# One layer's weight conversions name an activation table set, the order's model opens with no set loaded, and the plan's constants change with it

## The chip, the cores and the metric

The kernel runs on one core of a Trainium2 chip. The time is the device time of one execution in microseconds, the median of several runs. The core has five engines that run side by side, each taking its own instructions in order: PE (TensorE, matrix products), DVE (VectorE), ACT (ScalarE), POOL (GpSimd) and SP (SyncE, which here only issues DMAs). They wait for each other by semaphores. Data lie in SBUF (128 partitions), products in eight PSUM banks.

## The reference

Three steps follow each other; `B, H, S, D = 4, 8, 768, 48`, so there are 3072 tokens of 384 features.

```python
for t in range(S):                                   # attention with a decaying state
    state = alpha[:, :, t, :, None] * state + k_t v_t^T
    y[:, :, t] = q_t . state
h = x @ w_in                                         # layer one, 384 -> 2048 -> 384
P = a[0] + a[1] * h + a[2] * h2 + a[3] * h3          # h2 = h * h, h3 = h2 * h
Q = 1.0 + np.abs(b[0]) * np.abs(h) + np.abs(b[1]) * h2
x = (P / (Q + 1e-06)) @ w_out
h = x @ w_in2                                        # layer two, same sizes
out = (h * np.tanh(softplus(h))) @ w_out2
```

The weights arrive as 64-bit floats, so each is read as pairs of 32-bit words and made into two 32-bit parts, a high one in PE's reduced format and a low rest. Activations are split alike, and each product is the sum of three matmuls (high by high, high by low, low by high).

## The kernel before

**Tiling.** Tokens go in six chunks of 512 (128 positions of each of four batches). Attention works a chunk as two units (`attn_unit`): a tree of decay products, six levels of small score matmuls (L462) with a masked copy behind each (L497, or L486 and L492 on ACT) and a scaling of queries and keys (L477), then transposes (L526), outer products (L541), a state update (L550 on POOL, L555 on DVE) and the outputs (L576, L612). A layer works a chunk as 16 steps, one for each 128 of the 2048 hidden features. A step has nine hidden matmuls of 128x512 (L653) into one of three banks, the nonlinear function (`hidden`), a split of its result into high part `gh` and low part `gl` (`split_g`) and nine output matmuls (L702) that add into three banks over the 16 steps.

**Phases.** A pair (layer, chunk) is a phase. `PHASES` gives their order: (0, 0), (0, 1), (1, 0), (0, 2), (1, 1) and so on, layer two following layer one by a chunk. The attention of chunk c + 1 is worked beside the phases before layer one needs it; that of chunk 0 stands ahead of everything. Layer one's function takes ACT's logarithm and exponential, layer two's its Mish; these belong to two table sets, and ACT loads one at each change of layer (L690, L800; 1283 ns each). The first load, L731, stands in `start`.

**The order.** No order is written out by hand. Each operation is entered in a `Plan` with its engine, a length, a due time, the keys it reads and writes, and the code that emits it. `Plan.order` simulates the engines: when one is free, it takes the operation with the earliest due time of those that are ready. The sequence that results is what is emitted, for each engine in that order. So due times only rank what is ready, but one length that changes can change who is ready first, and with that the rest of the sequence. ACT operations may name a table set; where it isn't the one that the simulation holds loaded, their length is taken 1.4 us longer (line 157). Matmuls with constants (`warm`, L746) that feed nothing are put in where PE is idle until a set point; a trace shows 120 of them.

**Weight conversions.** `load_w` brings a pair of weight blocks in (L327 on SP) and converts it: ACT scales the high words (L328); then in form `A` of `E_CV` ACT makes two more pieces (L341, L342) and DVE joins them (L344), in form `D` DVE does three operations (L330, L332, L334). `E_HC` says whether ACT (L221) or DVE (L223) casts the high part, `E_LW` who makes the low part. Conversions 0 to 15 are layer one's, 16 to 31 layer two's. For later chunks the results are kept in DRAM and streamed back (`stream`, eight buffers each).

**Who does what.** Strings with a letter for each chunk give engines: `E_M` the multiplication in layer one's function (`V`: L671 on DVE, `P`: L675 on POOL), `E_GL0` and `E_GL1` the subtraction for `gl` in layer one and two (L214 on DVE, L216 on POOL). `T_PH` spaces the due times of a phase's steps, `AT_P` places the attention units, `D_SPL` and `LAG` place the split and the output matmuls behind a step, `W_LEAD` and `X_LEAD` the loads of streamed weights and of layer two's input, `D_W2` layer two's conversions, `D_X` the split of the inputs, `D_EV` the copies out of the output banks.

Of the kernel before, what the change touches and what calls it, by code (L numbers as in the profile page):

```python
# [14 lines left out]
AF = mybir.ActivationFunctionType  # L15
# [21 lines left out]
NLVM = 5  # L37
T0 = 24.974
PHASES = ((0, 0), (0, 1), (1, 0), (0, 2), (1, 1), (0, 3), (1, 2), (0, 4), (1, 3), (0, 5), (1, 4), (1, 5))
T_PH = (8.402, 4.683, 4.572, 7.535, 7.065, 5.706, 9.463, 9.341, 5.182, 6.904, 4.724, 3.344)  # L40
AT_P0 = (0.318, -13.418, 0.649)
AT_P1 = (0.292, 1.189, 0.288)
AT_P = (0.573, 0.916, 0.31)
D_MID = 10.219
LAG = (32.081, 10.172)
D_SPL = (-7.368, 6.936)
W_LEAD = 4.738
X_LEAD = 96.57
D_W1 = (0.495, 18.655)
D_W2 = (17.835, 18.763)  # L50
E_LO = 'VV'
E_TREE, E_QK = ('PPPVPV', 'VVVVVP')
E_M = 'PPPPPV'
E_GL0 = 'PVVPVV'
E_GL1 = 'VVVVPV'
R_PSUM = 'R.....'
NWL, NWO = 8, 8
N16 = 20
C_PED = 2
N_PRE = 8  # L60
E_LW = 'PVPPPVVVVVVVVVVVVVVVVVVVVVVVVVVV'
E_HC = 'AAVVVVVVAAVAAAAVVVAVAVAAVVVAVAAA'
E_X0 = 'V'
E_CV = 'ADAAAAAAAAAAADADDDDDADDDAAAAAAAA'
R0 = (39.706, 10.751)
NRAW, NF32 = 2, 2
D_X = 86.568
D_EV = -19.693
PAD_FROM = 290.0
PAD = 0.7  # L70
PAD_L = 0.5
F_OPEN = 3.25
F_END = 91.927
F_RATE = 1325.024
# [4 lines left out]
F64_SHIFT = 2.0 ** -112  # L79


class Plan:
# [32 lines left out]
    def order(self):  # L115
# [8 lines left out]
        ops = self.ops = list(ops)  # L124
        events = [(1.9, 1, n) for n in range(len(ops)) if not left[n]]
        heapq.heapify(events)
        out, busy, loaded = [], {}, "ln"
        fill, filler = self.fill, None
        while events:
            t = events[0][0]  # L130
            while events and events[0][0] <= t + 1e-9:
                _, kind, n = heapq.heappop(events)
# [13 lines left out]
            for eng, q in ready.items():  # L146
# [3 lines left out]
                while q:  # L150
                    due, n = heapq.heappop(q)
# [3 lines left out]
                    _, us, _, _, _, lock, after, table = ops[n]  # L155
                    if table and table != loaded:
                        us, loaded = us + 1.4, table
# [31 lines left out]
def attention_moe_kernel(ctx: ExitStack, tc: tile.TileContext,  # L189
                         qka, nat, consts, ab, w1i, w1o, w2i, w2o, out):  # L190
    nc = tc.nc
# [13 lines left out]
    def act(n, due, reads, writes, emit, src="p", ptr=0, table=None):  # L205
        plan.add("ACT", (0.075 if src == "p" else 0.115) + 0.000840 * n + 0.093 * ptr, due, reads, writes, emit, table=table)
# [101 lines left out]
    def load_w(src, l, key, j, due):  # L308

        n = nload[0]  # L310
        nload[0] += 1
        raw, st = raws[n % len(raws)], f32s[n % len(f32s)]
        kr, ks = f"raw{n % len(raws)}", f"f32{n % len(f32s)}"
# [11 lines left out]
        n = 2 * DM  # L325
        nth = nload[0] - 1
        dma(786, R0[nth] if nth < len(R0) else due - 6, [], [kr], lambda: nc.sync.dma_start(out=raw, in_=src[j]))  # L327
        act(n, due, [kr], [ks], lambda: nc.scalar.activation(st, mag, AF.Copy, scale=F64_SHIFT), src="s")  # L328
        if E_CV[nth] == "D":
            dve(n, due, [], [ks], lambda: nc.vector.tensor_scalar(  # L330
                out=si, in0=si, scalar1=3, scalar2=None, op0=ALU.logical_shift_left), fast=True)
# [556 lines left out]
```

## Time and profile before

| what | value |
|---|---|
| median of three runs | 1003.24 us (1002.68 to 1008.17) |
| the profiled execution | 1004.26 us, span 1001.6 us |
| PE busy | 969.1 us, 97% of the span |
| DVE, ACT, POOL busy | 668.6, 622.4, 263.6 us |
| DMA, mean over the span | 200 GB/s |
| mean granted TensorE clock | 0.989 |

The span is the time from the first instruction's start to the last one's end on the core; the execution's own time is 2.7 us longer. A row of busy time by stretch gives the stretch in us from the span's start, its length, the busy time of PE, PEld (weight loads of PE), DVE, ACT and POOL, each with its count of instructions, then the mean granted clock as a share of full speed, the DMA engines' busy share and GB/s. A row of the timeline gives the start, the duration, the engine, the line, the operation with what it writes and reads, and in brackets the idle time of the engine before it and who ended it ("issue": nothing that the profile shows). A row of waits gives who waited for whom, the total in us, how often, and the longest. A row of a group gives its busy time, the mean ns of one, and the idle time before it. The first hidden matmul of the phases, in order, starts at 85.48, 174.50, 257.10, 342.13, 409.41, 492.09, 560.89, 646.52, 719.17, 798.09, 859.06 and 928.42 us, and the stretches are cut there.

### The profile page before, as it was taken

Reading aid. Unit: us, or ns where it says so; the run is one execution under the profiler, and the core shown is the slowest. Engines: PE = TensorE matmul, PEld = TensorE weight load, DVE = VectorE, ACT = ScalarE, POOL = GpSimd, SP = SyncE. Lnnn points to the kernel's source line nnn. Section 1 sums busy time; section 2 is a strip of 40 time slices with the busy share of each in tenths; the row PEclk is TensorE's granted clock in tenths of the full one; section 3 lists DMA queues with packets and bytes.
Section 4 is the critical chain, followed back from the end, with each engine's and each line's share of the span. In section 5 each row is a group of like instructions: output and inputs, shape, how many; then the busy total and the mean of one; then the engine's idle time right before and its main releaser. Section 6 shows DMA issues by size and latency. Waiting matters only on the chain.

```text
span 1001.6 us, 24480 instructions
## 1 busy us (share of the span) xinstructions
PE 969.1 (97%) x10376; PEld 784.4 (78%) x10376; DVE 668.6 (67%) x867; ACT 622.4 (62%) x1051; POOL 263.6 (26%) x202
## 2 busy tenths in 40 slices
PE   7998999899999999999999999999999999999998
PEld 5776877678788878788878888878788878888886
DVE  5668799999997789954589634699952389400211
ACT  2587999699969698622399723396621299633332
POOL 3023675454100044200277700153300000133000
PEclk9799999999999999999999999999999999999999
DMA  7266549756588868557736764848456454565530
GB/s 293 98 222 270 199 151 326 252 164 206 203 292 311 309 230 277 173 191 225 255 97 222 228 210 135 293 153 263 117 167 190 143 156 143 142 214 150 172 111 31
DMA packets 75756, 199.98 MB, mean 200 GB/s; under 512 B 8192, under 2 KB 34944, under 8 KB 74112
## 3 DMA queue, kind: packets, MB, share of 16 engines
q1 hardware_dynamic: 75648, 198.43, 60.3%
q8 instruction: 81, 1.33, 0.5%
q14 instruction: 27, 0.22, 0.1%
HBM read 166.94 MB, written 31.46 MB: 198 GB/s over the span
## 4 chain that ended last, share of the span: by engine, by line
PE 68%; DVE 11%; ACT 9%; issue 3%; DMA 3%; POOL 1%; DVEq 0%; ACTq 0%; POOLq 0%
PE bank L702 31%; PE bank L653 30%; PE pair L462 4%; DVE zp L686 2%; DVE zp L677 1%; DVE zp L679 1%; DVE gg L214 1%; ACT zp L674 1%; DVE qka L477 1%; PE pair L612 1%; ACT u L668 1%; DMA qka<-in_qka_dram 1%; ACT gg L221 1%; ACT zp L681 1%; POOL zp L675 1%
## 5 line engine op out<-in xcount | busy, mean ns | idle before, releaser
L702 PE MATMUL bank<-gg,wo 128*128 128x512 f32 x1728 | 428.5, 392 | 1.9 <-DVE gg L214 0.8
L702 PEld LDWEIGHTS bank<-gg,wo 128*128 128x128 f32 x1728 | 321.0, 188 | 70.4 <-DVE gg L214 1.5
L653 PE MATMUL bank<-xh,wih 128*128 128x512 f32 x576 | 230.8, 401 | 4.9 <-DVE zp L679 2.3
L653 PE MATMUL bank<-xl,wih 128*128 128x512 f32 x576 | 225.6, 392 | 2.3 <-DVE xl L647 2.3
L653 PE MATMUL bank<-xh,wl 128*128 128x512 f32 x576 | 225.9, 392 | 0.5 <-DVE wl L214 0.5
L690 ACT ACTIVATE zp<-bank 128x512 f32<-128x512 f32 x96 | 57.4, 597 | 197.7 <-PE bank L653 196.1
L675 POOL TENSOR_TENSOR zp<-zp,u 128x512 f32<-128x512 f32 x80 | 125.2, 1571 | 160.0 <-ACT zp L674 159.5
L214 DVE TENSOR_TENSOR gg<-zp,gg 128x512 fp32r<-128x512 f32 x144 | 101.6, 710 | 95.3 <-ACT gg L221 90.4
L653 PEld LDWEIGHTS bank<-xh,wih 128*128 128x128 f32 x576 | 108.7, 189 | 30.2 <-DVE zp L679 2.7
L653 PEld LDWEIGHTS bank<-xl,wih 128*128 128x128 f32 x576 | 108.9, 189 | 24.4 <-DVE xl L647 3.1
L653 PEld LDWEIGHTS bank<-xh,wl 128*128 128x128 f32 x576 | 108.6, 189 | 24.1 <-DVE wl L214 1.0
L216 POOL TENSOR_TENSOR gg<-zp,gg 128x512 fp32r<-128x512 f32 x48 | 69.8, 1456 | 217.9 <-ACT gg L221 209.5
L221 ACT CAST gg<-zp 128x512 fp32r<-128x512 f32 x144 | 89.2, 621 | 46.2 <-PE bank L702 31.4
L550 POOL TENSOR_TENSOR tmp<-X,qk 48x768 f32<-48x768 f32 x19 | 30.3, 1595 | 232.3 <-DVE X L555 148.8
L677 DVE SCALAR_TENSOR_TENSOR zp<-zp,sc,bank 128x512 f32<-128x512 f32 x96 | 70.9, 742 | 22.3 <-ACT zp L676 19.8
L686 DVE SCALAR_TENSOR_TENSOR zp<-zp,sc 128x512 f32<-128x512 f32 x80 | 75.5, 949 | 6.4 <-ACT zp L685 5.5
L681 ACT ACTIVATE zp<-zp,c 128x512 f32<-128x512 f32 x96 | 69.4, 725 | 14.3 <-POOL zp L675 14.2
L462 PEld LDWEIGHTS pair<-qka 48*64 48x64 f32 (+4 forms) x3840 | 55.1, 129 | 27.8 <-issue 11.1
L676 ACT ACTIVATE zp<-bank,sc 128x512 f32<-128x512 f32 x96 | 66.1, 688 | 13.4 <-PE bank L653 10.3
L679 DVE SCALAR_TENSOR_TENSOR zp<-zp,sc,bank 128x512 f32<-128x512 f32 x96 | 71.1, 744 | 2.5 <-ACT u L668 0.7
L462 PE MATMUL pair<-qka 48*64 48x32 f32 (+4 forms) x3840 | 62.0, 215 | 6.2 <-DVE AT L497 3.3
L668 ACT ACTIVATE u<-bank 128x512 f32<-128x512 f32 x96 | 56.8, 596 | 15.8 <-PE bank L653 12.1
(124 smaller groups left out, 983.3 us busy)
## 6 DMA issues: line engine op xcount, KB each, us to landing
wo<-woD SPq DMA_DIRECT2D x160, 384.0 KB, 3.3
wl<-wlD SPq DMA_DIRECT2D x160, 192.0 KB, 2.5
qka<-in_qka_dram SPq DMA_DIRECT2D x10, 1536.0 KB, 7.8
woD<-wo SPq DMA_DIRECT2D x16, 768.0 KB, 4.9
raw<-in_w1o_dram SPq DMA_DIRECT2D x8, 768.0 KB, 4.9
raw<-in_w1i_dram SPq DMA_DIRECT2D x8, 768.0 KB, 5.2
wlD<-wl SPq DMA_DIRECT2D x16, 384.0 KB, 4.6
raw<-in_w2i_dram SPq DMA_DIRECT2D x8, 768.0 KB, 5.6
```

What stands on the lines that cost most here:

```text
L214: dve(n, due, reads, writes, lambda: nc.vector.tensor_tensor(**kw()))
L216: pool(n, due, reads, writes, lambda: nc.gpsimd.tensor_tensor(**kw()))
L221: act(n, due, reads, writes, lambda: nc.scalar.copy(out=out(), in_=in_()), src="s")
L462: nc.tensor.matmul(bk[j][o:o + m, 32 * g:32 * g + 32].rearrange("p (n l) -> p n l", l=L), lhsT=K[h, e * HC:e * HC + m], rhs=Qv[h, e, :, 1, :],
L653: nc.tensor.matmul(bank[hb], lhsT=w[:, k * P:(k + 1) * P], rhs=x[k], start=(k == 0 and j == 0), stop=(k == KT - 1 and j == 2))
L668: act(NTOK, due, [kh, "tab"], [ku], lambda: nc.scalar.activation(u, h, AF.Abs), table="ln")
L675: pool(NTOK, due, [ku], [kz], lambda: nc.gpsimd.tensor_tensor(out=zs[r], in0=zs[r], in1=u, op=ALU.mult))
L677: dve(NTOK, due, [kh], [kp], lambda: nc.vector.scalar_tensor_tensor(out=ps[r], in0=ps[r], scalar=A2, in1=h, op0=ALU.add, op1=ALU.mult), po ...
L679: dve(NTOK, due, [kh], [kp], lambda: nc.vector.scalar_tensor_tensor(out=ps[r], in0=ps[r], scalar=A1, in1=h, op0=ALU.add, op1=ALU.mult), po ...
L681: act(NTOK, due, [], [kz], lambda: nc.scalar.activation(zs[r], zs[r], AF.Ln, bias=c_1), src="s", ptr=1, table="ln")
L686: dve(NTOK, due, [kw], [kp], lambda: nc.vector.scalar_tensor_tensor(out=ps[r], in0=ps[r], scalar=A0, in1=w(), op0=ALU.add, op1=ALU.mult), ...
L702: nc.tensor.matmul(bank[5 + k], lhsT=wos[b][:, w, k * P:(k + 1) * P], rhs=x[q], start=(f == 0 and j == 0), stop=(f == FT - 1 and j == 2))
```

## The change

`Plan.order` opens with the table set `LOADED0`, which is `None`, in place of `"ln"`. Layer one's conversions (L328) name the set `"ln"`; layer two's name none. The loop that emits the operations still opens with `loaded = "ln"` (line 797). The constants that set due times and engines change as shown. No operation is added or left out, but for the five conversions whose form changes.

```diff
--- before.py
+++ after.py
@@ -37,38 +37,39 @@
 NLVM = 5
 T0 = 24.974
 PHASES = ((0, 0), (0, 1), (1, 0), (0, 2), (1, 1), (0, 3), (1, 2), (0, 4), (1, 3), (0, 5), (1, 4), (1, 5))
-T_PH = (8.402, 4.683, 4.572, 7.535, 7.065, 5.706, 9.463, 9.341, 5.182, 6.904, 4.724, 3.344)
+T_PH = (8.402, 4.739, 4.796, 7.6, 7.065, 5.962, 9.494, 9.394, 5.212, 7.04, 4.831, 2.283)
 AT_P0 = (0.318, -13.418, 0.649)
 AT_P1 = (0.292, 1.189, 0.288)
-AT_P = (0.573, 0.916, 0.31)
+AT_P = (0.576, 0.985, 0.276)
 D_MID = 10.219
-LAG = (32.081, 10.172)
-D_SPL = (-7.368, 6.936)
-W_LEAD = 4.738
-X_LEAD = 96.57
+LAG = (31.971, 10.172)
+D_SPL = (-1.971, 5.762)
+W_LEAD = -3.689
+X_LEAD = 69.333
 D_W1 = (0.495, 18.655)
-D_W2 = (17.835, 18.763)
+D_W2 = (20.572, 23.284)
 E_LO = 'VV'
 E_TREE, E_QK = ('PPPVPV', 'VVVVVP')
-E_M = 'PPPPPV'
-E_GL0 = 'PVVPVV'
-E_GL1 = 'VVVVPV'
+E_M = 'PPVPPV'
+E_GL0 = 'PVVVVV'
+E_GL1 = 'VPVPPV'
 R_PSUM = 'R.....'
 NWL, NWO = 8, 8
 N16 = 20
 C_PED = 2
 N_PRE = 8
 E_LW = 'PVPPPVVVVVVVVVVVVVVVVVVVVVVVVVVV'
-E_HC = 'AAVVVVVVAAVAAAAVVVAVAVAAVVVAVAAA'
+E_HC = 'AAVVVVVVAAVAAAAAAAAVVAAAAVVVVAVV'
 E_X0 = 'V'
-E_CV = 'ADAAAAAAAAAAADADDDDDADDDAAAAAAAA'
+E_CV = 'ADAAAAAAADAAADADDDDDADDDAADDDADA'
 R0 = (39.706, 10.751)
 NRAW, NF32 = 2, 2
-D_X = 86.568
-D_EV = -19.693
+D_X = 75.469
+D_EV = -9.067
 PAD_FROM = 290.0
 PAD = 0.7
 PAD_L = 0.5
+LOADED0 = None
 F_OPEN = 3.25
 F_END = 91.927
 F_RATE = 1325.024
@@ -124,7 +125,7 @@
         ops = self.ops = list(ops)
         events = [(1.9, 1, n) for n in range(len(ops)) if not left[n]]
         heapq.heapify(events)
-        out, busy, loaded = [], {}, "ln"
+        out, busy, loaded = [], {}, LOADED0
         fill, filler = self.fill, None
         while events:
             t = events[0][0]
@@ -325,7 +326,8 @@
         n = 2 * DM
         nth = nload[0] - 1
         dma(786, R0[nth] if nth < len(R0) else due - 6, [], [kr], lambda: nc.sync.dma_start(out=raw, in_=src[j]))
-        act(n, due, [kr], [ks], lambda: nc.scalar.activation(st, mag, AF.Copy, scale=F64_SHIFT), src="s")
+        act(n, due, [kr], [ks], lambda: nc.scalar.activation(st, mag, AF.Copy, scale=F64_SHIFT), src="s",
+            table="ln" if l == 0 else None)
         if E_CV[nth] == "D":
             dve(n, due, [], [ks], lambda: nc.vector.tensor_scalar(
                 out=si, in0=si, scalar1=3, scalar2=None, op0=ALU.logical_shift_left), fast=True)
```

## Rows read from the trace of the kernel before

**Rows 1.** Start in stretches: length, busy PE PEld DVE ACT POOL, clock, DMA, GB/s.

```profile
...
4.00:20.00 16.00, 14.97 (x351) 11.80 (x352) 10.17 (x12) 1.05 (x2) 7.69 (x10) 1.00 1.01 411
...
20.00:22.62 2.62, 0.00 (x0) 0.00 (x0) 1.84 (x2) 1.86 (x3) 1.44 (x3) 1.00 0.29 107
...
22.62:37.50 14.88, 14.88 (x217) 12.08 (x216) 8.58 (x10) 2.65 (x3) 0.00 (x0) 0.54 0.29 108
...
37.50:85.48 47.98, 43.45 (x1143) 34.48 (x1141) 36.02 (x42) 40.87 (x67) 8.27 (x9) 1.00 0.58 208
...
```

**Rows 2.** Timeline of the start: start us, duration, operation, idle before it in brackets.

```profile
...
10.34 0.91 ACT L328 ACTIVATE f<-raw 128x768 f32<-128x768 f32 x1 [6.20 <-DMA raw<-in_w1o_dram]
...
11.28 0.72 DVE L330 TENSOR_SCALAR f<-f 128x768 int32<-128x768 int32 x1 [0.82 <-ACT f L328]
...
12.04 0.96 DVE L332 SCALAR_TENSOR_TENSOR f<-raw,f 128x768 int32<-128x768 int32 x1
...
12.91 1.26 DVE L471 TENSOR_TENSOR qka<-qka 128x1024 f32<-128x1024 f32 x1
...
19.17 0.48 PE L746 MATMUL bank<-cst 128*128 128x256 f32 x1
...
22.62 1.24 PE L746 MATMUL bank<-cst 128*128 128x256 f32 x5 [2.96 <-issue]
...
```

**Rows 3.** Busy time by stretch between the phases' first hidden matmuls, and the sum.

```profile
...
0.00:85.48 85.48, 73.44 (x1709) 58.51 (x1709) 58.45 (x69) 48.18 (x77) 17.61 (x25) 0.92 0.60 221
...
85.48:174.50 89.02, 84.79 (x1265) 66.71 (x1258) 77.76 (x92) 82.33 (x139) 53.71 (x40) 0.98 0.63 223
...
174.50:257.10 82.60, 76.47 (x918) 60.94 (x919) 77.69 (x96) 69.89 (x131) 38.16 (x30) 0.98 0.63 207
...
342.13:409.41 67.28, 66.66 (x714) 53.71 (x709) 60.56 (x82) 58.59 (x101) 27.69 (x17) 1.00 0.79 257
...
409.41:492.09 82.68, 81.79 (x837) 66.45 (x835) 49.10 (x71) 24.52 (x43) 10.98 (x10) 1.00 0.65 205
...
492.09:560.89 68.80, 67.75 (x774) 54.54 (x772) 58.33 (x64) 60.62 (x104) 43.93 (x29) 1.00 0.60 187
...
798.09:859.06 60.97, 59.46 (x262) 48.91 (x261) 52.69 (x79) 54.88 (x97) 0.00 (x0) 1.00 0.51 149
...
928.42:1001.60 73.18, 69.52 (x307) 57.24 (x305) 12.37 (x18) 21.76 (x36) 1.29 (x1) 0.99 0.34 103
...
sum 1001.60, PE 969.11 PEld 784.45 DVE 668.59 ACT 622.38 POOL 263.64; mean PE 74.55 PEld 60.34 DVE 51.43 ACT 47.88 POOL 20.28
...
```

**Rows 4.** Waits of PE in phase (0, 1): total us, times, longest.

```profile
...
PE pair L462 <- DVE AT L497: 1.6, 2, 1.3
...
PE pair L462 <- DVE qka L477: 1.5, 1, 1.5
...
```

**Rows 5.** Waits of PE in the whole span, for the split results.

```profile
...
PE bank L702 <- DVE gg L214: 0.8, 1, 0.8
...
PE bank L702 <- POOL gg L216: 0.7, 1, 0.7
...
```

**Rows 6.** Line 686 by shape, in phase (0, 1), then in (0, 2).

```profile
...
L686 DVE SCALAR_TENSOR_TENSOR zp<-zp,sc 128x512 f32<-128x512 f32 x13 | 14.8, 1142 | 0.0
...
L686 DVE SCALAR_TENSOR_TENSOR zp<-zp,sc 128x512 f32<-128x512 f32 x13 | 10.5, 823 | 0.0
...
```

**Rows 7.** Groups of the whole span by shape: busy us, mean ns, idle before.

```profile
...
L671 DVE SCALAR_TENSOR_TENSOR zp<-zp,sc,u 128x512 f32<-128x512 f32 x16 | 11.9, 748 | 1.7 <-ACT zp L670 1.6
...
L341 ACT ACTIVATE zb<-raw 128x768 f16<-128x768 f32 x22 | 23.7, 1079 | 0.1
...
L342 ACT ACTIVATE zb<-raw,c_f 128x768 uint16<-128x768 uint16 x22 | 25.7, 1169 | 0.1
...
L344 DVE SCALAR_TENSOR_TENSOR f<-f,zb 128x768 int32<-128x768 int32 x22 | 24.1, 1095 | 14.0 <-ACT zb L342 10.7 <-ACT f L328 3.1
...
L223 DVE CAST wo<-f 128x768 fp32r<-128x768 f32 x8 | 4.5, 564 | 0.1
...
```

## The prediction

> **What bounds the kernel now.** I read the busy shares of the whole span first, then busy time cut at the first hidden matmul of each phase, then what PE waits for, and last the timeline of the start. The sum row has PE busy 969.11 of 1001.60 us [rows 3], so all that a new order could win from an idle PE is 32.5 us. The stretches say where it lies: 85.48 - 73.44 = 12.0 us before the first hidden matmul, 89.02 - 84.79 = 4.2 in phase (0, 0), 82.60 - 76.47 = 6.1 in (0, 1), 73.18 - 69.52 = 3.7 in the last stretch, whose end is the output's way out. That leaves 32.5 - 26.0 = 6.5 us for the other eight phases [rows 3]. From about 260 us on the kernel is bound by its matmuls. In (0, 1) DVE is busy 77.69 of 82.60 us, 94%, and PE's waits there are for DVE's attention work, 1.6 and 1.5 us [rows 3, 4]. Before 85.48 us PE has little real work: that stretch is bound by the attention of the first chunk, a chain through DVE, ACT and PE.
>
> The diff leaves every matmul in place. It moves 16 multiplications and 48 subtractions between DVE and POOL, nine casts between ACT and DVE, gives five weight conversions their other form, and changes due times, which only rank operations that are ready on one engine.
>
> **The start.** The order's model now thinks ACT's first conversion 1.4 us longer. On the chip nothing is loaded there for it, because the loop that emits still opens with the set loaded; ACT would have had 6.20 us idle ahead of it anyway [rows 2]. What can change is DVE's order: L330 at 11.28 and L332 at 12.04 (0.72 and 0.96 us) run before the attention's L471 at 12.91 [rows 2]. If they come later, that chain is up to 1.7 us earlier. I don't count this: PE stops in the midst of a group of fillers that depend on nothing, 2.96 us up to 22.62 [rows 2], after a stretch in which the DMA share is 1.01 [rows 1], and the same first loads are issued in the same order. Whoever arrives earlier waits there. The two operations then fill DVE's gap behind it. [...] I take 0.
>
> **Conversions.** One of the first layer (number 9) goes from the form with two more ACT operations to the one with three DVE operations. ACT saves 1.08 + 1.17 = 2.25 us [rows 7]; DVE gives 0.72 + 2 x 0.96 (the third is of the shape and kind of the second) for 1.10 [rows 2, 7], so +1.5. Number 15's cast goes from DVE (0.56 [rows 7]) to ACT (0.84, an estimate at 1.5 times that row). Phase (0, 0) has ACT at 82.33 and DVE at 77.76 of 89.02 us [rows 3]: ACT -1.4, DVE +1.0. Taken at a third of ACT's: -0.5, between -1.4 and +1.0. The other four reformed conversions and most moved casts belong to the second layer and fall behind 257 us, where PE is full: 0.
>
> Casts 16 and 17 go from DVE to ACT, and fall in (0, 1), where DVE is the fuller engine: 2 x 0.56 = -1.1. Second-layer conversions also get due 2.7 and 4.5 us earlier, and one more could slip into (0, 1) and cost DVE up to about 4 us (three operations as above, a cast and a subtraction). Taken: -1.1, between -1.1 and +4.
>
> **Engines in the layer-one phases.** In (0, 2) POOL loses its 16 multiplications and DVE gets them, 16 x 0.748 = +12.0 us [rows 7]. Against that stands contention: L686 takes 1142 ns in (0, 1), where POOL is busy 38.16 us, and 823 in (0, 2), where it is busy 27.69 [rows 3, 6]; the same engine's L671 of like shape takes 748 in a phase without POOL [rows 7]. So L686 gets back 13 x (823 - 748) = 1.0. DVE would stand at 60.56 + 12.0 - 1.0 = 71.6 us for a stretch of 67.28 [rows 3]. It fits only if attention work slides into (1, 1), where DVE is idle 82.68 - 49.10 = 33.6 us [rows 3]. Phase (0, 5), which has both operations on DVE already, runs at 52.69 of 60.97 us DVE with 1.5 us of PE idle [rows 3], so the step chain itself keeps pace. I take 0; bounds -0.6, all of PE's idle time there (67.28 - 66.66), and +8.9, worked out below.
>
> In (0, 3) the 16 subtractions go from POOL to DVE. That is the assignment that (0, 2) has now, with 0.6 us of PE idle against 1.1 in (0, 3) [rows 3]: 0, between -1.1 and +2. The subtractions that go to POOL lie in layer two, with DVE at 59% in (1, 1): 0.
>
> [...]
>
> **Due times.** Splitting the activations of layer one comes due 5.4 us later, so attention operations due in between pass it. That helps the waits of PE on attention in (0, 1), 1.6 + 1.5 = 3.1 us [rows 4]; what may suffer is PE's wait for the split results, so far 0.8 + 0.7 us in the whole span [rows 5]. Between -3.1 and +3, twice what is there now; I take -1.0, a third of the gain. Streamed weights come due 8.4 us later on SP's queue and the input of layer two 27 us later. PE waits for no transfer after the first constants, and eight buffers are in rotation: 0. The hold is that later loads queue up behind others on SP; a hidden matmul would then wait on a transfer.
>
> **Sum.** 0 - 0.5 - 1.1 + 0 + 0 - 1.0 = -2.6 us. The profiled execution took 1004.26 us, so 1001.7 by it; it lies 1.0 above the median of the runs, 1003.24, and on that median the forecast is 1000.6.
>
> **Rivals.** (a) The start opens: the stop before 22.62 and the slow clock behind it go, since PE's instruction count up to there changes with the order. For it: the stop is bound to a place in PE's stream, not to a dependency. Against: the loads that fill the DMAs stay. Price -7.1: 1003.2 - 7.1 = 996.1, and with the small terms 993.5. (b) The later splits clear the two DVE- and ACT-bound phases: of the 4.2 + 6.1 = 10.3 us PE idle, two thirds go, -6.9, so 996.3. For it: ACT and DVE at 92 and 94% with PE waiting on attention. Against: the listed waits on attention add to only 3.1. (c) Slower: DVE becomes the bound in (0, 2). If its 71.6 us can't slide and DVE fills 94% as in (0, 1), the stretch takes 71.6 / 0.94 = 76.2, +8.9, and with the other terms 1003.2 + 8.9 - 2.6 = 1009.5. It decides once more than 0.94 x 67.28 = 63.2 us of DVE work is tied to that stretch; the step chain alone, five operations at L671's 0.748 in 16 steps, is about 59.8 [rows 7]. Against: the 33.6 us idle in (1, 1). (d) Permutation only: the new order changes nothing that ends last, 1003.2.
>
> **Chances and range.** What can be told from no change in this kernel is about 0.5%, 5 us: under 998.2 is faster, over 1008.3 slower. Forecast 0.43 (own range 998.2 to 1004), (a) 0.20, (b) 0.16, (c) 0.14, (d) 0.07. Faster 0.36, same 0.50, slower 0.14. The range takes in (a) and (b) at their prices and reaches to (c): 992 to 1009.
>
> **What would show it.** Right: the first hidden matmul within a microsecond of 85.5, (0, 0) plus (0, 1) two to three us under 171.6, the rest unmoved. For (a): no idle of PE near 20 us, clock near 1.00 up to 37, hidden matmuls from about 78. For (b): these two phases at 165 or less. For (c): DVE over 94% in (0, 2) and PE waits on zp there. Wrong outright if PE waits on a transfer of wl, wo or xg, or if a second slow-clock stretch opens in the first 85 us.

## The result, and the profile after

The kernel after takes 988.63 us (median of 4 runs, 988.1 to 990.45) against 1002.96 for the kernel before beside it (4 runs, 999.71 to 1008.17): a ratio of 0.9851, interval 0.9821 to 0.9881. That is 14.3 us faster, where 2.6 were forecast and 992 was the low end of the range. The profiled execution took 988.1 us, its span is 986.3. Below the conversions of the weights a line number of before has become that number plus 2 (L471 is L473, L746 is L748); above them, and for L328 itself, it is plus 1 (L214 is L215). A kernel of the experiments that adds lines shifts the numbers further.

Two numbers split the 15.3 us between the spans. First the mean granted clock of the span, of the kernel before and then of the kernel after:

```profile
...
core 0: 1001.6 us, clock 0.989
...
```

```profile
...
core 0: 986.3 us, clock 0.998
...
```

Of full speed 0.011 x 1001.6 = 11.0 us were missing, and 0.002 x 986.3 = 2.0 us are missing now. So some 9.0 us of the gain are matmuls that run at a granted clock of 1.00 where they ran at 0.50, an estimate from these means. In the kernel before a 128x256 filler started 0.216 us after the one ahead of it at 1.00, and 0.427 us at 0.50 (medians). The rest is idle time of PE: 1001.6 - 969.1 = 32.5 us before [rows 3], 986.3 - 959.75 = 26.6 now, 5.9 us less. The kernel before scatters with its clock: 82 more executions, timed beside the experiments, took 997.9 to 1011.1 us with a granted clock from 0.984 to 0.995, median 0.991. Against that median the clock's part is 7 us. All four executions of the kernel after have 0.998.

The places come from busy time between the first hidden matmuls of the phases, here of the kernel after; its columns are those of [rows 3], its first line is the start and its last the end of the span:

```profile
...
0.00:76.92 76.92, 66.00 (x1639) 52.99 (x1639) 54.59 (x68) 46.63 (x76) 17.99 (x25) 0.98 0.68 247
76.92:168.39 91.47, 85.18 (x1332) 67.42 (x1326) 86.15 (x97) 83.36 (x141) 56.17 (x40) 1.00 0.61 220
168.39:239.87 71.48, 68.91 (x834) 54.69 (x833) 65.91 (x85) 63.73 (x120) 32.16 (x27) 1.00 0.66 217
239.87:329.09 89.22, 89.08 (x986) 72.31 (x984) 86.06 (x112) 63.78 (x107) 10.36 (x7) 1.00 0.80 286
329.09:396.55 67.46, 67.32 (x715) 54.88 (x714) 65.13 (x91) 59.08 (x104) 2.04 (x1) 1.00 0.77 249
396.55:478.18 81.63, 81.49 (x837) 66.53 (x835) 41.18 (x57) 23.26 (x41) 29.29 (x25) 1.00 0.67 212
478.18:547.32 69.14, 68.82 (x777) 54.92 (x775) 59.99 (x77) 60.37 (x105) 27.27 (x21) 1.00 0.63 197
...
782.85:843.81 60.96, 59.45 (x262) 48.91 (x261) 52.11 (x78) 54.91 (x97) 1.26 (x1) 1.00 0.52 149
...
913.17:986.30 73.13, 69.52 (x307) 57.24 (x305) 12.47 (x18) 21.75 (x36) 1.30 (x1) 1.00 0.34 103
sum 986.30, PE 959.75 PEld 777.63 DVE 663.80 ACT 610.24 POOL 256.48; mean PE 73.83 PEld 59.82 DVE 51.06 ACT 46.94 POOL 19.73
...
```

- The start is 8.56 us shorter (85.48 to 76.92). A part of that is work that crossed its border: 70 matmuls fewer stand ahead of it (1639 against 1709), 64 of them attention's, and 67 more in (0, 0). That is some 2 us, an estimate: PE's busy time fell by 7.4 us there, and 10.2 us less at half clock make 5.1 of it.
- The four phases (0, 0), (0, 1), (1, 0), (0, 2) together went from 89.02 + 82.60 + 85.03 + 67.28 = 323.9 to 91.47 + 71.48 + 89.22 + 67.46 = 319.6, 4.3 less. Taken one by one they mislead: (0, 1) lost 11.1, and (0, 0) and (1, 0) grew by 2.4 and 4.2, because work crossed their borders. PE's idle time in the four fell by 2.0 us (11.1 to 9.1), and two stretches of 3.4 us at half clock, shown below, are gone. The one in (0, 0) comes and goes: five of the seven kernels after whose order was frozen have one near 92 us again, with (0, 0) at 92.9.
- (1, 1) to (0, 4) went from 309.8 to 307.3, 2.5 less. From (1, 3) on nothing moved.
- DVE's work moved to earlier phases, not to later ones. It is busy 86.06 us in (1, 0), where it was 71.65, and 41.18 in (1, 1), where it was 49.10. Up to the start of (1, 1) its idle time went from 63.3 to 38.7 us.

The start itself, kernel after, in the windows and columns of [rows 1]:

```profile
...
4.00:20.00 16.00, 14.57 (x286) 11.34 (x287) 8.87 (x10) 1.00 (x2) 6.79 (x12) 0.93 1.01 409
20.00:22.62 2.62, 2.62 (x51) 2.02 (x49) 2.08 (x3) 0.50 (x1) 0.00 (x0) 0.77 0.25 93
22.62:37.50 14.88, 12.59 (x353) 10.13 (x347) 13.27 (x16) 9.21 (x14) 0.00 (x0) 1.00 0.34 114
37.50:76.92 39.42, 36.00 (x990) 29.28 (x976) 28.53 (x37) 34.10 (x58) 11.00 (x9) 1.00 0.72 254
...
```

Between 20 and 22.62 PE was idle throughout [rows 1], and now it is busy throughout. From 22.62 to 37.5 the granted clock was 0.54 and is 1.00; DVE gets 13.27 us of work done there instead of 8.58. Before, the clock stood at 0.50 for 13.65 us from 23.9 on; now the whole span has one such stretch, 3.4 us at 17.8. The timeline says what is left of the stop (columns as in [rows 2]):

```profile
...
10.01 0.93 ACT L329 ACTIVATE f<-raw 128x768 f32<-128x768 f32 x1 [5.94 <-DMA raw<-in_w1o_dram]
...
12.22 1.23 DVE L473 TENSOR_TENSOR qka<-qka 128x1024 f32<-128x1024 f32 x1 [0.52 <-PE pair L464]
13.36 1.30 DVE L499 COPY_PREDICATED AT<-cst,pair 128x512 f32<-128x512 int32 x1
14.46 0.98 DVE L334 SCALAR_TENSOR_TENSOR f<-raw,f 128x768 int32<-128x768 int32 x1
...
16.96 1.24 PE L464 MATMUL pair<-qka 48*64 48x32 f32 x59 [1.43 <-issue]
...
```

L334 (was L332, at 12.04, ahead of the attention's L471) now runs behind L473 and L499. PE's longest stop in this stretch that waits for nothing shown is 1.43 us and ends at 16.96; it was 2.96 and ended at 22.62 [rows 2]. These are two places in PE's stream: the first had a stop of 0.69 us before, and at the second there is none now ("What opened the start").

PE's waits on attention in phase (0, 1), kernel after (total us, times, longest), against [rows 4]:

```profile
...
PE pair L464 <- ACT AT L494: 1.1, 1, 1.1
PE pair L464 <- DVE qka L479: 1.0, 1, 1.0
PE pair L464 <- DVE AT L499: 0.2, 1, 0.2
...
```

And in the whole span, on the split results that POOL makes, against [rows 5]:

```profile
...
PE bank L704 <- POOL gg L217: 0.5, 1, 0.5
...
```

3.1 us on DVE have become 1.2, with 1.1 on ACT beside it. The later splits did not lengthen PE's wait for them (0.7 to 0.5 us for POOL's).

### The profile page after: what moved, and what is told of

It reads as the page before. It is cut to its first block, busy times and chain, and to the rows that moved or that the text cites. A ratio compares the mean times of both kernels' runs of the same rounds, so it can differ in the third digit from the quotient of the medians.

```text
span 986.3 us, 24509 instructions
## 1 busy us (share of the span) xinstructions
PE 959.7 (97%) x10370; PEld 777.6 (79%) x10370; DVE 663.8 (67%) x876; ACT 610.2 (62%) x1042; POOL 256.5 (26%) x202
## 4 chain that ended last, share of the span: by engine, by line
PE 77%; DVE 5%; ACT 2%; issue 1%; DMA 0%; POOL 0%; DVEq 0%
PE bank L704 36%; PE bank L655 35%; PE pair L464 3%; PE pair L614 2%; PE pair L528 1%; DVE zp L688 1%; PE pair L543 1%; DVE zp L679 1%; DVE zp L681 1%; DMA x2d<-u 0%; DVE qka L479 0%; ACT u L670 0%; DVE f L334 0%; DVE gg L224 0%; DVE gg L215 0%
## 5 line engine op out<-in xcount | busy, mean ns | idle before, releaser
L217 POOL TENSOR_TENSOR gg<-zp,gg 128x512 fp32r<-128x512 f32 x64 | 90.5, 1415 | 266.1 <-ACT gg L222 123.3
L215 DVE TENSOR_TENSOR gg<-zp,gg 128x512 fp32r<-128x512 f32 x128 | 92.4, 728 | 87.1 <-ACT gg L222 86.5
L677 POOL TENSOR_TENSOR zp<-zp,u 128x512 f32<-128x512 f32 x64 | 99.9, 1565 | 140.0 <-ACT zp L676 139.8
L655 PEld LDWEIGHTS bank<-xh,wih 128*128 128x128 f32 x576 | 108.1, 188 | 27.5 <-DVE zp L681 3.8
L679 DVE SCALAR_TENSOR_TENSOR zp<-zp,sc,bank 128x512 f32<-128x512 f32 x96 | 70.9, 742 | 12.5 <-ACT zp L678 12.1
L224 DVE CAST gg<-zp 128x512 fp32r<-128x512 f32 x48 | 23.2, 489 | 73.1 <-ACT zp L692 68.2
```

The lines of the kernel that those rows point to most:

```text
L215: dve(n, due, reads, writes, lambda: nc.vector.tensor_tensor(**kw()))
L217: pool(n, due, reads, writes, lambda: nc.gpsimd.tensor_tensor(**kw()))
L655: nc.tensor.matmul(bank[hb], lhsT=w[:, k * P:(k + 1) * P], rhs=x[k], start=(k == 0 and j == 0), stop=(k == KT - 1 and j == 2))
L677: pool(NTOK, due, [ku], [kz], lambda: nc.gpsimd.tensor_tensor(out=zs[r], in0=zs[r], in1=u, op=ALU.mult))
L679: dve(NTOK, due, [kh], [kp], lambda: nc.vector.scalar_tensor_tensor(out=ps[r], in0=ps[r], scalar=A2, in1=h, op0=ALU.add, op1=ALU.mult), po ...
```

## The experiments

Each kernel was timed beside the kernel before, and its ratio is to that one, whose median was 1002.57 us for e1 to e4, 1002.25 for s1, s2, d1 and d2, 1004.09 for q1, q2, f1 and p2, and 1004.73 for p1 and g2 to g4. Differences of medians in the text are therefore good to 1 or 2 us, and where they are close the ratio decides. "Frozen" means that the planner's finished order is kept and only the named operation moves. One table holds what the verdicts rest on; the last four columns are from each kernel's profiled execution, whose own time can lie a few us from the median.

| kernel | median us | ratio to before | first hidden matmul | (0, 0) to (0, 2) | clock | PE idle |
|---|---|---|---|---|---|---|
| before | 1002.96 | 1 | 85.48 | 323.9 | 0.989 | 32.5 |
| after | 988.63 | 0.9851 [0.9821, 0.9881] | 76.92 | 319.6 | 0.998 | 26.6 |
| e1_table_only | 1007.99 | 1.0062 [1.0032, 1.0092] | 79.43 | 336.8 | 0.992 | 41.0 |
| e2_consts_only | 1006.46 | 1.0039 [1.0007, 1.0072] | 84.73 | 330.6 | 0.988 | 33.7 |
| e3_after_old_engines | 1010.12 | 1.0052 [1.0018, 1.0087] | 84.39 | 338.5 | 0.981 | 38.5 |
| e4_after_old_split | 997.92 | 0.9951 [0.9931, 0.9971] | 77.52 | 327.2 | 0.993 | 31.7 |
| p1_after_charge | 993.46 | 0.9897 [0.9854, 0.9941] | 79.07 | 319.7 | 0.998 | 27.2 |
| p2_after_charge | 1000.85 | 0.9983 [0.9950, 1.0016] | 75.27 | 326.0 | 0.988 | 31.0 |
| s1_before_swap | 1002.61 | 1.0004 [0.9980, 1.0028] | 86.97 | 324.2 | 0.987 | 32.2 |
| s2_after_unswap | 990.13 | 0.9864 [0.9827, 0.9901] | 77.77 | 322.1 | 0.997 | 28.1 |
| q1_after_late | 990.36 | 0.9860 [0.9837, 0.9884] | 78.01 | 320.9 | 0.996 | 27.7 |
| q2_before_late | 999.85 | 0.9961 [0.9938, 0.9983] | 79.55 | 326.2 | 0.991 | 29.4 |
| f1_before_fewer_fillers | 1003.10 | 0.9994 [0.9973, 1.0016] | 82.81 | 326.0 | 0.986 | 35.6 |
| d1_twice_01 | 1004.59 | 1.0018 [0.9995, 1.0040] | 77.09 | 338.0 | 0.991 | 36.5 |
| d2_twice_12 | 991.32 | 0.9887 [0.9843, 0.9931] | 78.29 | 320.4 | 1.000 | 27.5 |
| g2_after_mult_pool | 990.63 | 0.9862 [0.9827, 0.9898] | 76.43 | 321.0 | 0.998 | 26.7 |
| g3_after_sub_pool | 993.72 | 0.9894 [0.9854, 0.9933] | 76.89 | 321.6 | 0.993 | 29.6 |
| g4_no_sub_01 | 988.98 | 0.9846 [0.9810, 0.9882] | 75.97 | 319.8 | 0.998 | 24.8 |

### Which half of the change

**The table set alone**, with every constant and engine of before:

```
-        out, busy, loaded = [], {}, "ln"
+        out, busy, loaded = [], {}, LOADED0                       # None
-        act(n, due, [kr], [ks], ..., src="s")
+        act(n, due, [kr], [ks], ..., src="s", table="ln" if l == 0 else None)
```

> The kernel before with the table edit alone (the order's model opens with no set, layer one's conversions name one); all constants as before. Theory: the start is won by this edit alone, because the second DVE operation of the first conversion falls behind the attention's first two operations: first hidden matmul at 77 us in place of 85.5, PE's stop of 2.96 us near 20 us gone, about 994 to 996 us. Rival A, the constants do it all: first hidden matmul at 85 us, 1001 to 1004 us. Rival B, the old constants don't fit the new start and give it back later: first hidden matmul at 77 us but over 1000 us.

**The constants and engines alone**, with the model opening as before:

```
-LOADED0 = None
+LOADED0 = "ln"
```

> The kernel after with the order's model opening with the set loaded, so that the first operations stand as before; all new constants. Theory: the start is back, first hidden matmul at 85.5 us, and the later phases keep their gain of about 7 us: 996 to 998 us. Rival A, the constants do it all: 988 to 990 us. Rival B, the constants fit only the new start: 1000 us or more.

Both are slower than before, as rival B of each said. The table set alone does open the start (79.43, a gain of 6.05) and gives it back twice over. Busy time of the first three phases, table set alone, then the first and third phase with the constants alone (columns as in [rows 3]):

```profile
...
79.43:174.44 95.01, 87.26 (x1325) 69.17 (x1323) 82.99 (x92) 81.25 (x137) 55.38 (x40) 0.96 0.58 205
174.44:252.54 78.10, 70.30 (x837) 55.25 (x836) 72.67 (x88) 65.14 (x123) 35.10 (x28) 1.00 0.62 203
252.54:346.80 94.26, 88.59 (x922) 71.18 (x920) 80.92 (x104) 71.59 (x115) 9.73 (x8) 1.00 0.81 283
...
```

```profile
...
84.73:179.86 95.13, 87.14 (x1267) 69.48 (x1265) 86.77 (x97) 84.26 (x143) 55.36 (x40) 0.96 0.62 217
...
252.94:343.58 90.64, 87.02 (x910) 70.11 (x908) 82.91 (x107) 64.50 (x108) 7.77 (x7) 0.98 0.76 271
...
```

With the table set alone PE idles 7.8, 7.8 and 5.7 us in these phases; in the kernel after it is 6.3, 2.6 and 0.1. With the constants alone the start is hardly shorter (0.75), and (0, 0) and (1, 0) pay in idle time and in clock. So no half carries the gain; the two together make one order that does.

**After, with the engine assignments of before**, and **after, with the split's due times of before**:

```
-E_M = 'PPVPPV'      # and E_GL0, E_GL1, E_HC, E_CV
+E_M = 'PPPPPV'      # all five strings as before
```

> The kernel after with the five strings that give engines and conversion forms as before. Theory: the engines matter little, since layer one's later phases took the same time to within 0.4 us: 988 to 991 us. Rival: the casts and the conversions that left DVE and ACT in phases (0, 0) and (0, 1) are what these phases gained: 993 to 997 us, with (0, 1) at 80 us or more in place of 71.5.

```
-D_SPL = (-1.971, 5.762)
+D_SPL = (-7.368, 6.936)
```

> The kernel after with the due times of the activation splits as before (D_SPL). Theory: attention operations that may pass the splits are what shortens (0, 0) to (1, 0), 256.7 us before and 252.2 after; without it they go back to 255 to 257 and the time to 991 to 994 us. Rival: the splits' due time does nothing that can be measured, 987 to 990 us.

The engines put back cost 21.5 us, more than the whole gain and beyond both ranges expected; (0, 1) is at 80.33, as the rival said. In the profiled execution, the longest of this kernel's runs at 1016.55, the clock falls to 0.981, which is 0.019 x 1014.7 = 19.3 us of full speed missing. The splits put back cost 9.3 us, again beyond both ranges; by the profile 0.6 lies in the start and 7.5 in (0, 0) to (0, 2).

**A charge of 1.2 and of 1.6 us instead of 1.4** for a table set in the order's model; the chip's work is the same, the order alone differs:

```
-                        us, loaded = us + 1.4, table
+                        us, loaded = us + 1.2, table        # p2: 1.6
```

> The kernel after with the model's charge for a change of table set at 1.2 us in place of 1.4; on DVE the first 295 operations keep their order, so (0, 0) to (1, 0) begin as in the kernel after. Theory, the gain lies in the order of those phases: their times stay, later ones move by a microsecond or two either way, 986 to 992 us. Rival, any change of the model's lengths costs 10 us as 1.6 did: 997 us or more.

> The kernel after with the order's model charging 1.6 us in place of 1.4 for a change of table set; nothing else. It touches ten operations' lengths in the model and none on the chip. Theory: the constants fit one order only, and whatever changes the order early loses the gain in (0, 0) to (0, 2), as the part versions did: 995 to 1008 us. Rival: the gain is robust, 987 to 992 us.

0.2 us in a planner's constant costs 4.8 us (more than the theory allowed and less than the rival asked; the interval touches that of the kernel after) or 12.2 us. The larger charge has the shortest start of all (75.27) and loses it in single phases. Two of them are (0, 0), 91.47 in the kernel after, and (0, 4), 72.31 there (busy time by phase, columns as in [rows 3]):

```profile
...
75.27:169.99 94.72, 88.64 (x1391) 70.33 (x1390) 88.15 (x102) 86.92 (x145) 52.74 (x40) 0.96 0.63 224
...
636.62:716.02 79.40, 76.28 (x828) 61.06 (x823) 75.07 (x99) 53.90 (x90) 27.34 (x17) 0.96 0.57 177
...
```

Both have a clock of 0.96: 0.04 x 94.72 = 3.8 and 0.04 x 79.40 = 3.2 us.

### What opened the start

**Before, frozen, with L332 moved behind L471 and L497**, and **after, frozen, with the same operation moved back ahead of L473**:

```
+        out.remove(self.marks[('conv', 1)])
+        out.insert(out.index(self.marks[('copy', 0, 1)]) + 1, self.marks[('conv', 1)])   # s2: ahead of ('K', 0)
```

> The kernel before with every engine's order frozen and one DVE operation moved: the second operation of the first conversion (L332) stands behind the attention's L471 and the L497 that follows it. Theory: this swap is what wins the start, so the first hidden matmul comes at 77 to 80 us and the time is 994 to 998 us. Rival: PE's stop near 20 us and the slow clock behind it belong to PE's own order, which is unchanged here; the chain that arrives 1.7 us earlier waits there, first hidden matmul at 84 to 86 us, 1000 to 1004 us.

> The kernel after with every engine's order frozen and that DVE operation moved back ahead of the attention's two. Theory of the swap: first hidden matmul at 80 to 85 us in place of 76.9, 992 to 997 us. Rival, PE's own order decides: first hidden matmul within 1.7 us of 76.9, 988 to 990 us.

Neither moves the time. The start of the first in two windows of [rows 1]:

```profile
...
20.00:22.62 2.62, 0.18 (x1) 0.00 (x0) 2.37 (x3) 1.30 (x2) 1.96 (x3) 0.91 0.24 93
22.62:37.50 14.88, 14.63 (x214) 11.68 (x214) 7.91 (x10) 3.09 (x4) 0.00 (x0) 0.50 0.29 108
...
```

And PE's stop in its timeline (L754 is the fillers' L746):

```profile
...
22.87 2.29 PE L754 MATMUL bank<-cst 128*128 128x256 f32 x5 [2.69 <-issue]
...
```

The chain came earlier and waited at the same stop; the clock behind it is 0.50 as before. The swap of DVE's operations is the visible sign of the new order and not its cause.

**Before and after, frozen, with one early load moved behind a later one** (0.77 MB for chunk 3, on the queue of the first loads; issued at 26.10 us in place of 10.01 on the kernel after, at 28.30 in place of 10.33 on the kernel before, so 16 and 18 us later and not 12):

```
+        out.remove(self.marks[('q1', 6)])
+        out.insert(out.index(self.marks[('raw', 2)]) + 1, self.marks[('q1', 6)])
```

> The kernel after with its order frozen and one DMA moved: the 0.77 MB load of the fourth chunk's queries (L410, issued at 10.01 us and not used before 34) stands behind the next raw weight load, some 12 us later. Theory: PE's stops in the first 20 us come with the DMAs saturated by the first loads; 0.77 MB less is 1.9 us less of that at 410 GB/s, so PE's stop of 1.43 us shrinks and the first hidden matmul comes 0 to 2 us earlier: 986 to 989 us. Rival: the stops don't depend on the loads, 988 to 990 us.

> The kernel before with its order frozen and the same DMA moved. Theory: PE's stop of 2.96 us ends 1.9 us sooner or is gone, the slow clock behind it is shorter, and the first hidden matmul comes at 79 to 83 us: 996 to 1000 us. Rival: the stop belongs to PE's stream alone; first hidden matmul at 85 to 87 us, 1001 to 1004 us.

On the kernel before the stop and the slow clock behind it are gone in the profiled execution. Its start in the windows of [rows 1], then phase (0, 1) and a stretch of it:

```profile
...
4.00:20.00 16.00, 16.00 (x286) 12.34 (x286) 8.52 (x10) 0.98 (x2) 4.93 (x8) 1.00 0.93 377
20.00:22.62 2.62, 2.62 (x71) 2.07 (x71) 2.62 (x3) 1.88 (x3) 2.46 (x3) 1.00 0.03 9
22.62:37.50 14.88, 13.55 (x415) 11.12 (x415) 12.40 (x16) 8.48 (x14) 1.21 (x3) 0.99 0.43 161
...
167.69:253.36 85.67, 80.56 (x919) 64.21 (x919) 76.28 (x96) 70.08 (x131) 36.59 (x30) 0.92 0.59 199
187.20:197.40 10.20, 9.48 (x82) 7.32 (x83) 8.37 (x10) 6.81 (x13) 4.81 (x3) 0.50 0.65 233
...
```

The share of the DMAs up to 20 us goes from 1.01 [rows 1] to 0.93, PE is busy in all 16 us, and the first hidden matmul comes 5.9 us earlier. By the ratio 3.9 us come off the time, for in (0, 1) a new stretch of 10.2 us at half clock costs about 5. On the kernel after the same edit gives nothing.

What PE's stop ends with can be read from the traces, although its label is "issue". They hold the packets of a queue that the page calls `instruction`, here of the kernel after (packets, MB, share of the DMA engines):

```profile
...
q8 instruction: 81, 1.33, 0.6%
...
```

That is 16.4 KB a packet, and PE's 10370 matmuls with as many weight loads are 256 instructions, or 128 matmuls, to each. Count PE's matmuls from its first one: in all 18 traces the matmuls 224, 352, 480 and so on, every 128th, start at least 1.23 us after the packet of their turn has landed (ten places each, none sooner; 1.27 us at the least in the kernel before, 1.25 in the kernel after). All 38 idle times of PE over 0.3 us at these places in the first 60 us end 1.23 to 1.62 us after such a landing. So PE's stops there end with the landing of a packet; that the packet holds PE's next instructions is read from these counts, an estimate. Its landing moves with the first loads: with the one load moved the second packet landed at 19.80 us in place of 21.72 on the kernel after (q1). In the kernel before, the second packet landed at 21.23 us, and PE stood at matmul 352 from 19.66 to 22.62. In the kernel after it landed at 21.72, and matmul 352 started at 23.16, later than before and with no stop. What differs is the work between matmuls 224 and 352. Before, two fillers here and a third at 19.17 [rows 2]:

```profile
...
16.42 1.12 PE L462 MATMUL pair<-qka 48*64 48x32 f32 x61 [0.69 <-issue]
17.48 0.70 PE L746 MATMUL bank<-cst 128*128 128x256 f32 x2
...
```

After, ten:

```profile
...
18.13 3.93 PE L748 MATMUL bank<-cst 128*128 128x256 f32 x10
22.00 1.41 PE L464 MATMUL bank<-zp 48*64 48x32 f32 x62
...
```

They keep PE busy until the place can be passed, the longer since the clock is at half from 17.80 to 21.22. The kernels with three fillers there (before, e2, s1, f1) stop for 2.14 to 2.97 us at matmul 352 and run at half clock for 6.8 to 17.1 us behind it; the thirteen with seven or ten, e1 among them, idle there for 0.58 us at most. So the table set's charge, which e1 has and e2 has not, brings the fillers ahead of the place.

q2 has three and no stop, and two things differ in its profile. The second packet landed at 20.18 us, 1.05 sooner than before, which is the moved load. And PE came to matmul 352 only at 21.45 us: its ten fillers from 9.40 on took 4.27 us in this execution, where they took 2.42 in the kernel before. (The row above says 1.00, but this trace has no record of the clock before 13.2 us.) d2 and g4 begin as slowly with the start of the kernel after unchanged, so that is not the edit's doing. The moved load alone would leave some 2 us of the stop, an estimate from 2.96 - 1.05. That it takes the stop away by itself isn't shown, and no run moves fillers alone ahead of the place.

**Before, frozen, with 20 of the 120 filler matmuls left out** (they only keep PE busy):

```
     def warm():
+        warmed[0] += 1
+        if 18 < warmed[0] <= 28:
+            return
```

> The kernel before with its order frozen and 20 of its 120 filler matmuls left out, those that ran at half clock from 25.50 to 29.28 and from 32.57 to 37.87 us. They feed nothing, so no result changes. Theory: at half clock these fillers hold the attention's score matmuls up; without them the first hidden matmul comes 2 to 5 us earlier, 997 to 1001 us. Rival: the attention chain is set by DVE there, or the clock stays low for longer without them: first hidden matmul at 85 to 90 us, 1002 to 1007 us.

The same window of the start:

```profile
...
22.62:37.50 14.88, 11.18 (x266) 9.34 (x265) 9.86 (x12) 4.54 (x8) 0.00 (x0) 0.50 0.30 109
...
```

The stop stays (2.97 us) and the clock stays at 0.50, for 17.1 us. The start is 2.7 us shorter, and the later phases take it back. Fewer fillers, here behind the stop, are not what opened the start.

### What bounds the phases behind it

**After, frozen, with the 16 subtractions of one phase issued twice on DVE**, some 11 us of added work, in (0, 1) and in (1, 2):

```
+        if (l, c) == (0, 1):                # d2: (1, 2)
+            def twice():
+                for _ in range(2):
+                    nc.vector.tensor_tensor(out=gls[q], in0=ps[r], in1=ghs[q].bitcast(F32), op=ALU.subtract)
+            dve(NTOK, due, [kp, kgh], [kgl], twice)
+            return
```

> The kernel after with its order frozen, and the DVE subtraction of the activation split issued twice in each of the 16 steps of phase (0, 1): 11 us more DVE work there. Theory: to the end of (0, 2) the kernel is bound by DVE, which is busy over 92% in each stretch from 77 to 397 us, so most of it shows: 995 to 1000 us. Rival: these phases are bound by PE and the attention chain, and DVE's idle takes it up: 988 to 992 us.

> The same doubling in the 16 steps of phase (1, 2), 547 to 631 us, where DVE is busy less than half of the time: 11 us more DVE work. Both theories: nothing to measure, 988 to 990 us. If it costs as much as in (0, 1), the doubling lengthens each step's own chain and says nothing of DVE as a bound.

**After, frozen, with those subtractions left out in (0, 1)** (the low part of the split isn't formed there):

```
+        if (l, c) == (0, 1):
+            dve(NTOK, due, [kp, kgh], [kgl], lambda: None)
+            return
```

> The kernel after with its order frozen and the 16 DVE subtractions of phase (0, 1) left out, so that the low part of the activations of that chunk isn't formed and its matmuls read what the buffers hold. DVE does 11 us less there. Theory of a bound shared by DVE and PE: adding DVE work there costs its whole length, but taking it away gives no more than PE's idle there, 2.6 us in (0, 1) and what waits at its ends: 985 to 988 us. Rival, DVE alone is the bound to the end of (0, 2): 978 to 982 us.

Phases (0, 1) and (1, 0), first with the work doubled, then with it left out:

```profile
...
170.03:251.07 81.04, 72.75 (x834) 56.66 (x833) 75.68 (x94) 63.24 (x119) 32.06 (x27) 0.96 0.58 191
251.07:347.56 96.49, 91.62 (x986) 73.25 (x985) 93.17 (x120) 64.91 (x108) 9.08 (x7) 0.98 0.74 264
...
```

```profile
...
168.90:239.32 70.42, 68.61 (x834) 54.92 (x833) 57.91 (x73) 63.48 (x120) 30.66 (x27) 1.00 0.67 220
239.32:328.29 88.97, 88.83 (x986) 72.36 (x984) 84.21 (x108) 64.01 (x107) 9.32 (x7) 1.00 0.80 287
...
```

11 us more of DVE in (0, 1) cost 16 us of time, more than the 995 to 1000 us of the theory: 9.6 there and 7.3 in (1, 0), with the clock down to 0.96 and 0.98. Three stretches of 3.4 us at half clock, at 185, 202 and 267 us, are 5.1 of that, and the rest is about the added work itself. 8 us less (57.91 against 65.91) give nothing (988.98 against 988.63 us, where up to 3 were expected): (1, 0) behind it has PE busy 88.83 of 88.97 us. In (1, 2) the same added work costs 0.8 us of the phase (84.95 against 84.18); 1.4 of the 2.7 us by which this kernel is slower lie in its start, where nothing was edited. So up to (1, 0) DVE is a bound on one side only: the new order sits where the load of DVE and of PE both just fit.

**After, frozen, with the multiplications of (0, 2), and with the subtractions of (0, 3), back on POOL**:

```
+        (lambda: nc.gpsimd.tensor_tensor(out=zs[r], in0=zs[r], in1=u, op=ALU.mult)) if c == 2 else ...
```

> The kernel after with its order frozen and the 16 multiplications of phase (0, 2) back on POOL, ACT's operation ahead of them in the form that goes with it. DVE loses 12 us there. Theory, engines count for little since PE is busy 67.32 of that stretch's 67.46 us: 988 to 991 us. Rival, DVE on this edit is part of the gain, since POOL's slower step delays the results: 993 us or more, with (0, 2) over 69 us.

```
+        if (l, c) == (0, 3):
+            dve(NTOK, due, [kp, kgh], [kgl], lambda: nc.gpsimd.tensor_tensor(..., op=ALU.subtract))
+            return
```

> The kernel after with its order frozen and the 16 subtractions of phase (0, 3) back on POOL. Theory, engines count for little: (0, 3) within 1 us of 69.1 and 988 to 991 us. Rival: (0, 3) over 71 us and 992 us or more.

With the multiplications on POOL (0, 2) takes 69.03 us against 67.46, and (1, 1) 83.12 against 81.63. The other frozen kernels after repeat these two phases within 0.1 us, so the 3.1 us are clear; of the time only 2.0 us show, and there the two ratios' intervals overlap. With the subtractions on POOL the median is 5.1 us higher, and not by their own phase, which stays at 69.05. The profiled execution is the slowest of four (991.81 to 995.86); two with a clock of 0.997 and 0.998 took 991.8 and 992.3. Its loss is in (1, 2), 90.07 against 84.18. PE's timeline there, and the two windows around it with the columns of [rows 1]:

```profile
...
551.47 0.50 PE L655 MATMUL bank<-xl,wih 128*128 128x512 f32 x1 [1.91 <-DVE xl L649]
...
```

```profile
...
549.17:552.90 3.73, 1.82 (x8) 1.05 (x6) 3.69 (x5) 3.72 (x7) 2.84 (x4) 1.00 0.44 126
552.90:559.70 6.80, 6.22 (x15) 4.67 (x15) 5.70 (x6) 2.81 (x4) 4.23 (x6) 0.50 0.25 67
...
```

A wait of 1.91 us, and behind it 6.8 us at half clock although PE is busy 6.22 of them: 3.4 us of lost speed on top of the wait, which together are 5.3 of the 5.9.

## Why the prediction was wrong, point by point

**The failed step is "The start", taken at 0.** It measured -8.56. The text had the right place, the right stop and the right rival: (a), at -7.1, is what happened, and its signs came as named (no idle of PE near 20, clock 1.00 from 22.62 to 37.5, first hidden matmul at 76.92 for "about 78"). What failed is the choice between them, and the sentence on which it rested, "Whoever arrives earlier waits there". That sentence is true of an earlier chain (s1), and the place itself stayed: PE started its matmul 352 at 22.62 us before and at 23.16 after. But in the new order PE didn't arrive earlier. With ten fillers in place of three ahead of that matmul it came at 23.11, so neither the 2.96 us of idle time nor the 13.65 us at half clock behind them followed. (a)'s own argument, that the stop is bound to a place in PE's stream, was right. "The loads that fill the DMAs stay" was the one against it, and they did stay; the cost of the stop hung on what PE had to do until then, which the prediction didn't ask. The -7.1 counted what DVE could catch up between 20 and 37.5, its idle time of 2.62 - 1.84 + 14.88 - 8.58 = 7.1 us there [rows 1]. ACT caught up there too, 9.21 us of work against 2.65, and some 2 us crossed into (0, 0).

**The frame was too narrow.** "All that a new order could win from an idle PE is 32.5 us" leaves out the clock. 11.0 us of full speed were missing before, nearly all in three stretches at half clock (13.65 + 2 x 3.4 = 20.45 us, half of it lost). Each stands behind idle time of PE: the stop of 2.96 us, 2.0 of the 4.6 us before 95.6, and 1.6 of the 3.0 us before 177.5. 9.0 of the 11.0 us came back, more than the 5.9 from idle time. The second and third lie in (0, 0) and (0, 1). Kernel before, same columns as [rows 1]:

```profile
...
95.60:99.00 3.40, 3.40 (x71) 2.46 (x70) 2.86 (x4) 3.35 (x7) 1.27 (x1) 0.50 0.00 0
...
177.50:180.90 3.40, 3.40 (x10) 2.62 (x9) 2.89 (x5) 2.06 (x7) 1.04 (x1) 0.50 0.45 183
...
```

PE looks full in both, and so its busy time hid them.

**Conversions (-1.6) and due times (-1.0)** were right in sign and small: the four phases gave -4.3 in place of -2.6. Idle time of PE gives -2.0 and the two half-clock stretches, 6.8 us at half speed, -3.4; 62 more matmul records fall into these phases (3867 against 3805) and take some back. The due times could not be priced by themselves: undoing the split's alone costs 9.3 us (e4). Which single rank in the new order is worth how much stays open, since each undone part makes another order. The prediction put two changes at nothing without a word, the due times of the input splits (`D_X`, by 11.1 us) and of the copies out of the output banks (`D_EV`, by 10.6); no run undoes them by themselves.

**Engines, taken at 0.** In (0, 2) the length was right (67.28 to 67.46), and the reason was wrong in part. Groups of lines by shape, kernel after: the first in (0, 1), the next two in (0, 2), answering to [rows 6, 7].

```profile
...
L688 DVE SCALAR_TENSOR_TENSOR zp<-zp,sc 128x512 f32<-128x512 f32 x12 | 9.9, 833 | 1.0 <-ACT zp L687 0.8
...
L673 DVE SCALAR_TENSOR_TENSOR zp<-zp,sc,u 128x512 f32<-128x512 f32 x15 | 12.5, 833 | 1.4 <-ACT u L670 1.1 <-ACT zp L672 0.3
...
L688 DVE SCALAR_TENSOR_TENSOR zp<-zp,sc 128x512 f32<-128x512 f32 x14 | 10.5, 751 | 0.1
...
```

The added 12.0 us measured 12.5, and L688 got back to 751 ns as forecast. But DVE ended at 65.13, not 71.6, since attention work had moved ahead into (1, 0) and not back into (1, 1). The gain of the edit, 2 to 3 us (g2), appears as the loss that it avoids. For (0, 3) 0 was right for the phase and wrong for the time: 3 to 5 us (g3), in the profiled execution by way of (1, 2).

**Later phases, taken at 0**, measured -2.5, in (1, 1) and (1, 2) above all.

**The rivals.** (b) forecast 165 or less for (0, 0) plus (0, 1); they take 162.95. Its signs came too, yet most of that went over into (1, 0), so the four phases gained 4.3 and not 6.9. (c) asked for DVE over 94% in (0, 2); it has 65.13 of 67.46, 97%, and PE idles 0.14 us, so 94% was no point of decision. DVE as a bound does exist, in earlier phases: d1 pays 16 us for 11. (a) and the four phases' 4.3 together with the 2.5 behind them make the 15.3; they were held as rivals of one another and came together.

## What to carry to other kernels

Before pricing a new order, look at the granted clock stretch by stretch: full PE at half clock (20.45 us in the kernel before) is time to be won that no list of waits shows. With the lost speed behind it the wait of 1.91 us in g3 came to 1.91 + 3.4 = 5.3, and the stop of 2.96 us in the kernel before to some 2.96 + 13.65 / 2 = 9.8 (estimates). Where PE stops at a fixed place in its stream, as here at matmul 352, the time of that place may stay (22.62 us before, 23.16 after) and the stop still go: ask what a new order puts ahead of it. Where a planner writes the order, its constants and its cost model are one setting, and neither a half of such a change nor a step of 0.2 us in it can be expected to give a share of the whole.

## What the runs showed of the hardware

In the kernel before the granted clock was 0.50 for 13.65 us behind PE's wait of 2.96 us, and for 3.41 us each behind waits of 2.02 us (to 94.99) and 1.58 us (to 176.58); in the kernel after for 3.41 us behind one of 1.43 (to 16.96); in g3 for 6.8 us behind one of 1.91, with PE busy 91% of that time; in f1 for 17.1 us behind one of 2.97. What sets how long it stayed these traces don't show. The queue `instruction` brought 81 packets of 16.4 KB in the kernel after, one to each 128 of PE's matmuls with their weight loads, and in 18 traces every 128th matmul from the 224th on started 1.23 us or more after the packet of its turn had landed (ten places each).

In the kernel before, what a single L686 on DVE paid for running beside POOL in (0, 1) and (0, 2) was all or little, and it went with which of the two started first. The two-input L686 has a mean of 1142 ns in (0, 1) [rows 6], but none of the 13 takes that (least, median and longest in ns, first and last start in us):

```profile
...
L686 DVE SCALAR_TENSOR_TENSOR zp<-zp,sc x13: 740/747/1787, 199.7 to 246.0; 128x512 f32<-128x512 f32 x13
...
```

Five took 1753 to 1787 ns, and a POOL instruction was running when each of them started. The other eight took 740 to 747, three of them with a POOL instruction that began while they ran. So the mean of 823 in (0, 2) [rows 6] is one instruction of 1779 among 13, and the 833 of the kernel after in (0, 1) is one of 1782 among 12. With the multiplications of (0, 2) back on POOL seven of 14 grew, to between 1177 and 1878 ns; this group by shape:

```profile
...
L690 DVE SCALAR_TENSOR_TENSOR zp<-zp,sc 128x512 f32<-128x512 f32 x14 | 16.6, 1184 | 1.7 <-ACT zp L689 1.0
...
```

The kernel before had 823 there, with POOL busier (27.69 us against 22.85). So one L686 took up to 1787 - 740 = 1047 ns longer here when POOL was already running, and POOL's busy time did not tell how often the two met so.
